# Cross-covariance attention and highway layer in one kernel: twelve tiles of v transposed by DMA, and the last stores ordered in another way

## The chip, the cores and the metric

The kernel runs on one NeuronCore of a Trainium2 chip. The metric is device time in microseconds (us), the median of several executions of the same program. The core has a matrix engine (TensorE, in profiles PE, with its weight loads as PEld), VectorE (DVE), ScalarE (ACT) and GpSimd (POOL); SyncE (SP) mostly issues DMAs. Each engine works through its own instructions in their order and waits on semaphores for the others. All DMAs of the core share 16 DMA engines.

## The reference

For each of four batches of 6336 rows and 256 columns, q and k are normalised along the rows, a 256 x 256 matrix of their products goes through a softmax, and v is multiplied by it; the rows of all batches then go through a highway layer.

```python
B, N, C = (4, 6336, 256)
qn = q / (np.linalg.norm(q, axis=1, keepdims=True) + 1e-06)
kn = k / (np.linalg.norm(k, axis=1, keepdims=True) + 1e-06)
s = kn.transpose(0, 2, 1) @ qn / tau
a = np.exp(s - s.max(-1, keepdims=True))
a /= a.sum(-1, keepdims=True) + 1e-09
x = (v @ a).reshape(B * N, C)
H = np.maximum(x @ w_h, 0.0)
T = 1.0 / (1.0 + np.exp(-(x @ w_t + b_t)))
out = T * H + (1.0 - T) * x
```

Inputs and output are f32; the kernel computes its matrix products in f16 with f32 sums.

## The kernel before

**Tiles.** The rows of a batch are cut into 49 tiles of 128 rows and a rest of 64. A tile takes one row from each partition's stretch, so that a load of several tiles is one long run in each partition. Loads of q, k and v are issued by POOL and cast to f16 on the way; v of the last batch is loaded in four groups of 12, 12, 12 and 13 tiles.

**Two phases, interleaved.** Phase 1 of a batch (`p1_tile`) takes one tile of q and k at a time and adds to two PSUM banks: `S`, the products of k and q, and `G`, the squares on whose diagonals the norms lie. For some tiles of q ACT squares the values instead and DVE adds them up (`squares`, with the places in `SQ_RUNS`). After the last tile of a batch a chain of small steps (`chain`: norms, softmax, and the products of the attention matrix with the two weight matrices) gives `mr`, three 256 x 256 matrices. Its steps are placed at slots by `PLACES`; for the last batch that is `LAST`.

**Phase 2** runs in 100 slots, 25 for each batch, and each slot deals with a pair of tiles of v (the 25th of a batch with the last tile and the rest). A pair needs v transposed, since v is the stationary operand. `transpose` does this on PE: four transposes of 128 x 128 into `vt_bank`, one PSUM bank whose halves the pairs take in turn; `vt_copy` lets DVE copy the result to SBUF (`vts`). Then `mains` makes three groups of four matmuls: `zbank` (the gate), `h` and `x`. ACT takes the sigmoid of the gate into `tt` (`gate_act`) and writes the bias back into the bank for the gate two slots later (`seed`); for the slots in `PE_BIAS` two matmuls on PE do that instead. DVE makes two products, `th` and `ux` (`products`), and POOL subtracts them (`subtract`) into an output tile `o` that holds four slots, in a ring of six. Slots 98 and 99 are subtracted by DVE.

**What sets the order.** The order on each engine is written out by the loop over slots, `for t in range(NSLOT)`. Phase 1 tiles of the next batch are dealt out over the slots; `P1_END` says by which slot a batch must be through, for the last one 63, and from slot 75 on the slots are of the last batch. `TURNS` and `GATES` say in which slots no pair, or two, are transposed or have their gates computed, instead of one: so transposes run three or more slots ahead of `mains`, and gates up to four. A small planner (`note`, `next_loads`, with its constant of 0.305 us for a tile) decides in which slot POOL issues a load.

**Stores.** `subtract` puts a finished output tile into the list `stores`, and `send_store` issues the oldest on SP. Up to `DEFER` stores are kept back, one fewer from each of the slots in `DRAIN` on. A store of 1 MB holds four slots; slots 95 to 98 are stored one by one, 256 KB each, and slot 99 in two parts of 128 and 64 KB. A store is also tied to the latest subtraction that stands before it in the program (`behind`), whatever it holds:

```python
while len(stores) > room and out_now < 2:
    note(send_store(last), now)
    out_now += 1
...
while stores:
    send_store(None)
```

In slot 99 `last` is the subtraction of slot 99 itself, since the loop calls it before it sends the stores.

Of the kernel before, what the change touches and what calls it, by code (L numbers as in the profile page):

```python
# [12 lines left out]
f16 = mybir.dt.float16  # L13
u16 = mybir.dt.uint16

P = 128
# [3 lines left out]
def kernel(  # L20
# [19 lines left out]
    nc = tc.nc  # L40

    B, N, C = q.shape
# [8 lines left out]
    def spans(*sizes):  # L51
        got, s0 = [], 0
        for ns in sizes:
            got.append((s0, ns))
            s0 += ns
        assert s0 == NS
        return got
# [5 lines left out]
    QTILES = 8  # L63
    QRING = 6
    ORING = 6
    DEFER = 5
    DRAIN = [61, 75, 76, 81]
    VG = [spans(6, 10, 12, 12, 9)] + [spans(12, 12, 12, 13)] * (B - 1)
    VTILES = 13
    VALL = [(b, g) for b in range(B) for g in range(len(VG[b]))]  # L70
    VFIRST = [VALL.index((b, 0)) for b in range(B)]
    VRING = 4
    NPAIR = (NS + 1) // 2
# [8 lines left out]
    HEAD = sum(CHAIN0)  # L82
    P1_END = [18, 42, 63]

    GATES = {14: 2, 20: 0, 24: 2, 51: 2, 52: 2, 55: 2, 58: 0, 66: 0, 69: 0, 73: 0, 95: 2}
    TURNS = {50: 1, 51: 2, 52: 2, 59: 1, 61: 2, 64: 0, 70: 0, 73: 0, 93: 2}
    VTS = 9
    OLAST = 2
    TTS = 6

    PE_BIAS = (18, 68, 88, 97)

    DVE_SUBS = (98, 99)

# [2 lines left out]

    SQ_RUNS = {1: (6, 14, 21, 28), 2: (17, 26, 35), 3: (11, 23, 33)}  # L100
    SQ_TILES = 8
    SQ_CUTS = 4
    SQ_RATE = 2
# [1 line left out]

    EARLY = {"sums": (0, "pre"), "norms": (0, "pre"), "invs": (1, "pre"), "cq": (1, "pe"), "logits": (2, "pre"), "exps": (2, "post"), "softmax": (4, "pre"), "at": (4, "pe"), "at_copy": (5, "pre"), "ahat": (5, "pe"), "ahat_copy": (6, "pre")}
    MID = {"sums": (0, "pre"), "norms": (0, "pre"), "invs": (2, "pre"), "cq": (2, "pe"), "logits": (2, "post"), "exps": (3, "post"), "softmax": (3, "post"), "at": (5, "pe"), "at_copy": (6, "pre"), "ahat": (6, "pe"), "ahat_copy": (7, "pre")}
    LAST = {"sums": (0, "pre"), "norms": (0, "pre"), "invs": (2, "pre"), "cq": (2, "pe"), "logits": (2, "post"), "exps": (3, "pre"), "softmax": (6, "pre"), "at": (8, "pe"), "at_copy": (9, "pre"), "ahat": (9, "pe"), "ahat_copy": (10, "pre")}
    PLACES = [None, EARLY, MID, LAST]

    ctx.enter_context(tc.manual_schedule())
    const_pool = ctx.enter_context(tc.tile_pool(name="consts", bufs=1))
    stream_pool = ctx.enter_context(tc.tile_pool(name="stream", bufs=2))
# [9 lines left out]
    q_t, k_t, v_t = {}, {}, {}  # L123
# [76 lines left out]
    def hx_tile(name, shape=(P, 2, C), dt=f32):  # L200
        return psum_pool.tile(list(shape), dt, tag="hx", bufs=3, name=name)
# [39 lines left out]
    def squared(b, j):  # L241

        for n, j0 in enumerate(SQ_RUNS.get(b, ())):
            count = SQ_TILES - (n > 0)
# [10 lines left out]
    def squares(b, j):  # L255
# [24 lines left out]
        add_up(len(cuts))  # L280
        more = n < len(SQ_RUNS[b]) - 1
        if more:
# [12 lines left out]
    def add_up(k):  # L295
        while k > 0 and cuts:
            dst, source = cuts.pop(0)
            nc.vector.tensor_reduce(  # L298
                out=dst, in_=source, op=AluOp.add, axis=mybir.AxisListType.XY
            )  # L300
            k -= 1
# [220 lines left out]
    vT_t = {}  # L522
    vt_bank = psum_pool.tile([P, 2, 2, 2, P], f16, tag="vT", name="vt_bank")
    o_t = {}
    NSLOT = B * NPAIR

    def v_of(b, s):
# [2 lines left out]
        g = max(i for i in range(len(VG[b])) if VG[b][i][0] <= s)  # L530
        return v_t[VFIRST[b] + g][:, s - VG[b][g][0], :]

    def nrows(i):
        return [P, REM] if i == NPAIR - 1 else [P, P]

# [24 lines left out]
    def mains(t, dst, part, seeded):  # L560
        b, i = divmod(t, NPAIR)
        mr = mr_t[b]
        if t in PE_BIAS and seeded:
            for u in range(2):
                nc.tensor.matmul(
                    dst[:, u, :], ones_hl, bt_hl, start=(u == 0), stop=False,
                    skip_group_check=True,
                )
        for u, r in enumerate(nrows(i)):
            for kt in range(2):  # L570
                nc.tensor.matmul(  # L571
                    dst[0:r, u, :], vT_t[t][:, u, kt, 0:r], mr[:, part, kt, :],
                    start=(not seeded and kt == 0 and (u == 0 or i == NPAIR - 1)),
                    stop=(kt == 1 and (u == 1 or i == NPAIR - 1)),
                    skip_group_check=seeded,
                )
# [11 lines left out]
    stores = []  # L588
# [16 lines left out]
    def send_store(behind):  # L605

        tiles, parts = stores.pop(0)
        for dst, src in parts:
            dma = nc.sync.dma_start(out=dst, in_=src)
            if behind is not None:  # L610
                tc.add_manual_dep(
                    dma.ins, behind.ins.name,
                    mybir.DependencyInfo(
                        mybir.DependencyClass.Sync, mybir.DependencyReason.DATA
                    ),
                )
        return tiles
# [3 lines left out]
    def gate_act(s, z):  # L621
        tt_t[s] = work_pool.tile([P, 2, C], f32, tag="tt", bufs=TTS, name=f"tt{s}")
        nc.scalar.activation(out=tt_t[s], in_=z, func=Act.Sigmoid)  # L623

    def seed(s, z):
        if s + 2 < NSLOT and s + 2 not in PE_BIAS:
            nc.scalar.copy(out=z, in_=btb)  # L627
# [34 lines left out]
    def nominal_slot(n):  # L662

        if n < HEAD:
            return -1
        lo, base = RAMP, HEAD
        for i, e in enumerate(P1_END):
            if n < (i + 1) * (NS + 1):
                return lo + (n - base) * (e - lo) // ((i + 1) * (NS + 1) - base)
            lo, base = e + len(LULL) - 1, (i + 1) * (NS + 1)  # L670

    want = []
    for n in range(QFIRST[1] + 1, len(QALL)):
        b, g = QALL[n]
        at = nominal_slot((b - 1) * (NS + 1) + QG[b][g][0])
        for fn, key in ((load_q, "q"), (load_k, "k")):
            want.append((at, len(want), fn, n, ("q", n - QRING), QG[b][g][1]))
    for m in range(2, len(VALL)):
        b, g = VALL[m]
        at = b * NPAIR + VG[b][g][0] // 2 - LOOK - 1  # L680
# [16 lines left out]
    def note(tiles, now):  # L697
        dma_at[0] = max(dma_at[0], now) + tiles * TILE_US
# [96 lines left out]
    now = START_US  # L795
# [46 lines left out]
    def run(t, when):  # L842
        for fn in hooks.pop((t, when), []):
            fn()
# [4 lines left out]
    last = None  # L849
    for t in range(NSLOT):  # L850
        b, i = divmod(t, NPAIR)
        ready = set(used)
        slot[0] = t
        run(t, "pre")
        zs = range(zdone, min(NSLOT, zdone + GATES.get(t, 1)))
        zdone = zs.stop
        turned = range(tdone, min(NSLOT, tdone + TURNS.get(t, 1)))
        tdone = turned.stop
        for s in zs:
            mains(s, zbank[s % 2], 2, True)  # L860
            gate_act(s, zbank[s % 2])
        if pending:
            last = subtract(*pending.pop())
        for s in turned[:1]:
            vt_copy(s, transpose(s))
        for s in zs:
            seed(s, zbank[s % 2])
        h = hx_tile(f"h{t}")
        mains(t, h, 1, False)
        x = hx_tile(f"x{t}")  # L870
        mains(t, x, 0, False)
        for s in turned[1:]:
            vt_copy(s, transpose(s))
        run(t, "pe")
        pending.append((t, *products(t, h, x)))
        add_up(2 if len(cuts) > SQ_RATE else 1)
        run(t, "post")
        for s in turned:
            bb, ii = divmod(s, NPAIR)
            for g, (s0, ns) in enumerate(VG[bb]):  # L880
                if 2 * ii + 2 == s0 + ns or (g == len(VG[bb]) - 1 and ii == NPAIR - 1):
                    used.add(("v", VFIRST[bb] + g))
        if t == NSLOT - 1:
            last = subtract(*pending.pop())


        pb = done1 // (NS + 1)
        count = 0
        for s in turned:
            bb, ii = divmod(s, NPAIR)  # L890
            g = max(g for g in range(len(VG[bb])) if VG[bb][g][0] <= 2 * ii)
            now = max(now, landed.get((load_v, VFIRST[bb] + g), now))
        now += 1.5
        if pb < len(P1_END):
            left = P1_END[pb] - t
            if 0 <= t - end1 < len(LULL):
                due = LULL[t - end1]
            else:
                due = -(-((pb + 1) * (NS + 1) - done1) // left)
            for ahead in range(due):  # L900
                if left > 1 and tile_lands(done1 + ahead) > now + 0.43 * ahead:
                    break
                count += 1
        for _ in range(count):
            pb, j = divmod(done1, NS + 1)
            now = max(now, min(tile_lands(done1), now + 20.0)) + 0.43
            p1_tile(pb + 1, j)
            squares(pb + 1, j)
            done1 += 1
            if j == NS:  # L910
                end1 = t + 1
                steps = chain(pb + 1)
                for name, (at, when) in PLACES[pb + 1].items():
                    hooks.setdefault((t + 1 + at, when), []).append(steps[name])


        if t not in (end1 - 1, end1):
            next_loads(2, now)
        room = DEFER - sum(t >= at for at in DRAIN)
        out_now = 0  # L920
        while len(stores) > room and out_now < 2:
            note(send_store(last), now)
            out_now += 1
        vT_t.pop(t, None)
    while stores:
        send_store(None)
# [36 lines left out]
```

## Time and profile before

| | us |
|---|---|
| median of 5 runs | 275.68 |
| lowest and highest | 275.51, 275.82 |
| the profiled execution, its own time | 275.57 |
| its span, first to last instruction | 273.8 |

The granted TensorE clock was 0.991 on average. The stores are issued by SP; the 1 MB ones take 9.0 us from issue to landing in the middle, and 3.8 us where little else is on the DMA engines (issued at 255.0). The costliest groups of the last stage are, by line, the products `th` (L639) and `ux` (L644) on DVE, POOL's subtraction (L654), and on PE the matmuls of L571 and the transposes of L544.

In the profile an engine's line of digits shows how full it was in each fortieth of the span. A group's line gives line, engine, operation, what is written from what, and the times. In a timeline the first two columns are start and duration in us, and in brackets stands how long the engine had been idle and what ended that. Matmuls overlap, so that the step from one start to the next says more than a duration.

### The profile page before, as it was taken

Reading aid. Unit: us, or ns where it says so; the run is one execution under the profiler, and the core shown is the slowest. Engines: PE = TensorE matmul, PEld = TensorE weight load, DVE = VectorE, ACT = ScalarE, POOL = GpSimd, SP = SyncE. Lnnn points to the kernel's source line nnn. Section 1 sums busy time; section 2 is a strip of 40 time slices with the busy share of each in tenths; the row PEclk is TensorE's granted clock in tenths of the full one; section 3 lists DMA queues with packets and bytes.
Section 4 is the critical chain, followed back from the end, with each engine's and each line's share of the span. In section 5 each row is a group of like instructions: output and inputs, shape, how many; then the busy total and the mean of one; then the engine's idle time right before and its main releaser. Section 6 shows DMA issues by size and latency. Waiting matters only on the chain.

```text
span 273.8 us, 6875 instructions
## 1 busy us (share of the span) xinstructions
PE 253.6 (93%) x2759; PEld 224.9 (82%) x2759; DVE 204.6 (75%) x444; ACT 164.4 (60%) x291; POOL 171.8 (63%) x191
## 2 busy tenths in 40 slices
PE   0679898999999999999999999999999999999990
PEld 0569786999999988899999988899998887999870
DVE  0060046995896876679999767779999999999993
ACT  1030046777772485688675589586645986777750
POOL 6231350899646785628779575609656897888770
PEclk9999999999999999999999999999999999999996
DMA  6999999999999999999999999999999759993366
GB/s 124 212 215 212 210 210 208 214 214 212 215 212 212 215 217 210 236 311 246 286 287 244 305 244 224 219 303 268 279 285 348 154 152 299 423 362 158 156 253 236
DMA packets 16725, 65.64 MB, mean 240 GB/s; under 512 B 1843, under 2 KB 4150, under 8 KB 13750
## 3 DMA queue, kind: packets, MB, share of 16 engines
q0 software_dynamic: 11744, 39.13, 72.2%
q1 hardware_dynamic: 4950, 26.09, 23.9%
q8 instruction: 21, 0.34, 0.5%
q14 instruction: 10, 0.08, 0.1%
HBM read 78.38 MB, written 25.95 MB: 381 GB/s over the span
## 4 chain that ended last, share of the span: by engine, by line
PE 82%; DMA 10%; DVE 3%; issue 1%; ACT 1%; POOL 0%; DVEq 0%; ACTq 0%; POOLq 0%
PE zbank L571 16%; PE h L571 15%; PE x L571 15%; PE S L225 14%; DMA k<-in_k_dram 10%; PE vt_bank L544 8%; PE G L228 7%; PE G L231 4%; PE ah L464 1%; DVE ux L644 1%; DVE th L639 1%; PE sums L320 1%; PE cq L394 1%; DVE vts L557 0%; ACT ssb L417 0%
## 5 line engine op out<-in xcount | busy, mean ns | idle before, releaser
L654 POOL TENSOR_TENSOR o<-th,ux 128x512 f32<-128x512 f32 x95 | 120.6, 1280 | 41.6 <-DVE ux L644 20.4
L571 PEld LDWEIGHTS <-vts 128*128 128x128 f16 x1200 | 110.0, 98 | 14.6 <-issue 3.9
L623 ACT ACTIVATE tt<-zbank 128x512 f32<-128x512 f32 x100 | 59.1, 596 | 55.8 <-PE zbank L571 52.5
L225 PE MATMUL S<-q,k 128*128 128x256 f16 x392 | 81.9, 276 | 10.3 <-DMA k<-in_k_dram 10.3
L228 PE MATMUL G<-k 128*128 128x128 f16 x392 | 73.7, 221 | 0.0
L639 DVE SCALAR_TENSOR_TENSOR th<-h,tt 128x512 f32<-128x512 f32 (+1 forms) x104 | 69.1, 668 | 5.6 <-ACT tt L623 1.0
L644 DVE SCALAR_TENSOR_TENSOR ux<-tt,x 128x512 f32<-128x512 f32 (+1 forms) x104 | 68.1, 658 | 0.0
L571 PE MATMUL h<-mr,vts 128*128 128x256 f16 (+1 forms) x400 | 60.5, 273 | 0.0
L571 PE MATMUL x<-mr,vts 128*128 128x256 f16 (+1 forms) x400 | 60.5, 273 | 0.0
L571 PE MATMUL zbank<-mr,vts 128*128 128x256 f16 (+1 forms) x400 | 59.6, 273 | 0.0
L557 DVE COPY vts<-vt_bank 128x512 f16<-128x512 f16 x96 | 40.4, 421 | 22.9 <-PE vt_bank L544 22.6
L627 ACT COPY zbank<-btb 128x512 f32<-128x512 f32 x94 | 55.2, 592 | 2.7
L225 PEld LDWEIGHTS <-k 128*128 128x128 f16 x392 | 38.8, 99 | 14.7 <-DMA k<-in_k_dram 10.6
L228 PEld LDWEIGHTS <-k 128*128 128x128 f16 x392 | 38.8, 99 | 0.7
L544 PE MATMUL vt_bank<-ident,v 128*128 128x128 f16 x392 | 38.1, 219 | 0.2
L231 PE MATMUL G<-q 128*128 128x128 f16 x246 | 34.4, 222 | 0.0
L544 PEld LDWEIGHTS <-v 128*128 128x128 f16 x392 | 29.9, 98 | 3.3 <-issue 1.1
L129 POOL DMA_DIRECT2D q<-in_q_dram x28 | 15.9, 568 | 18.2 <-DMA q<-in_q_dram 5.8
L135 POOL DMA_DIRECT2D k<-in_k_dram x28 | 15.2, 542 | 16.6 <-DMA k<-in_k_dram 9.3
L273 ACT ACTIVATE sq<-q 128x512 f32<-128x512 f16 (+1 forms) x41 | 23.6, 619 | 0.0
L231 PEld LDWEIGHTS <-q 128*128 128x128 f16 x246 | 19.3, 100 | 1.6
L298 DVE TENSOR_REDUCE sq<-sq 128x64 f32<-128x512 f32 x28 | 18.0, 680 | 0.0
(100 smaller groups left out, 120.5 us busy)
## 6 DMA issues: line engine op xcount, KB each, us to landing
out_dram<-o SPq DMA_DIRECT2D x23, 1024.0 KB, 9.0
q<-in_q_dram POOLq DMA_DIRECT2D x20, 512.0 KB, 16.9
k<-in_k_dram POOLq DMA_DIRECT2D x20, 512.0 KB, 17.8
v<-in_v_dram POOLq DMA_DIRECT2D x11, 768.0 KB, 18.8
v<-in_v_dram POOLq DMA_DIRECT2D x3, 832.0 KB, 26.2
out_dram<-o SPq DMA_DIRECT2D x4, 256.0 KB, 2.3
q<-in_q_dram POOLq DMA_DIRECT2D x3, 320.0 KB, 17.4
k<-in_k_dram POOLq DMA_DIRECT2D x3, 320.0 KB, 17.0
```

What stands on the lines that cost most here:

```text
L225: nc.tensor.matmul(S[:, c, :], kc, qq[0:nr, :], start=first and c == 0, stop=last and c == 1)
L228: nc.tensor.matmul(G[:, c, :], kc, kc, start=first and c == 0, stop=False)
L231: nc.tensor.matmul(G[:, 2 + c, :], qc, qc, start=False, stop=last and c == 1)
L273: nc.scalar.activation(out=sq[:, o // 2, :, u : u + src.shape[1]].rearrange("p c u -> p u c"), in_=src, func=Act.Square,)
L544: nc.tensor.transpose(ps[:, u, c, 0 : nr[u]], vt[0 : nr[u], bass.ts(c, P)], ident[0 : nr[u], 0 : nr[u]],)
L557: nc.vector.tensor_copy(out=sb, in_=ps)
L571: nc.tensor.matmul(dst[0:r, u, :], vT_t[t][:, u, kt, 0:r], mr[:, part, kt, :], start=(not seeded and kt == 0 and (u == 0 or i == NPAIR - 1 ...
L623: nc.scalar.activation(out=tt_t[s], in_=z, func=Act.Sigmoid)
L627: nc.scalar.copy(out=z, in_=btb)
L639: nc.vector.scalar_tensor_tensor(out=th[pr, us, :], in0=h[pr, us, :], scalar=0.0, in1=tt[pr, us, :], op0=AluOp.max, op1=AluOp.mult,)
L644: nc.vector.scalar_tensor_tensor(out=ux[pr, us, :], in0=tt[pr, us, :], scalar=1.0, in1=x[pr, us, :], op0=AluOp.subtract, op1=AluOp.mult,)
L654: last = eng.tensor_tensor(out=ot[pr, o0 + us.start : o0 + us.stop, :], in0=th[pr, us, :], in1=ux[pr, us, :], op=AluOp.subtract,)
```

## The change

Two groups of six tiles of v of the last batch, tiles 26 to 31 and 38 to 43 (pairs 88 to 90 and 94 to 96), are no longer transposed by PE and copied by DVE. In slots 78 and 79 SP issues one DMA transpose for each, from the tile of v in SBUF into a tile in the rings of q and k, and the pairs' matmuls read that tile. In slots 98 and 99 stores are no longer tied to the latest subtraction, only to their own data; the last store, the 64 rows of the rest, is issued by ACT. Several constants move: the slots of `DRAIN`, `GATES`, `TURNS` and `PE_BIAS`, the first run of squares of the last batch, and the softmax of the last batch by one slot.

On the engines PE has 24 transposes and their weight loads fewer, DVE six copies fewer, SP two DMA transposes more and a store fewer, and ACT a store more. On SP the first transpose stands after the store of o62 and before that of o66, the second between those of o66 and o70.

```diff
-    DRAIN = [61, 75, 76, 81]
+    DRAIN = [57, 78, 74, 84]
...
-    GATES = {14: 2, 20: 0, 24: 2, 51: 2, 52: 2, 55: 2, 58: 0, 66: 0, 69: 0, 73: 0, 95: 2}
-    TURNS = {50: 1, 51: 2, 52: 2, 59: 1, 61: 2, 64: 0, 70: 0, 73: 0, 93: 2}
+    GATES = {17: 2, 20: 0, 27: 2, 51: 2, 52: 2, 55: 2, 58: 0, 66: 0, 69: 0, 73: 0, 95: 2}
+    TURNS = {49: 2, 51: 2, 52: 2, 53: 0, 59: 1, 60: 2, 64: 0, 72: 0, 73: 0, 93: 2}
...
-    PE_BIAS = (18, 68, 88, 97)
+    TGROUPS = ((26, 6, 78), (38, 6, 79))
+
+    PE_BIAS = (18, 21, 83, 97)
...
-    SQ_RUNS = {1: (6, 14, 21, 28), 2: (17, 26, 35), 3: (11, 23, 33)}
+    SQ_RUNS = {1: (6, 14, 21, 28), 2: (17, 26, 35), 3: (9, 23, 33)}
...
-    LAST = {"sums": (0, "pre"), "norms": (0, "pre"), "invs": (2, "pre"), "cq": (2, "pe"), "logits": (2, "post"), "exps": (3, "pre"), "softmax": (6, "pre"), "at": (8, "pe"), "at_copy": (9, "pre"), "ahat": (9, "pe"), "ahat_copy": (10, "pre")}
+    LAST = {"sums": (0, "pre"), "norms": (0, "pre"), "invs": (2, "pre"), "cq": (2, "pe"), "logits": (2, "post"), "exps": (3, "pre"), "softmax": (7, "pre"), "at": (8, "pe"), "at_copy": (9, "pre"), "ahat": (9, "pe"), "ahat_copy": (10, "pre")}
...
+    BY_DMA = {}
+
+    def dma_transposes(t):
+
+        for n, (s0, ns, at) in enumerate(TGROUPS):
+            if at != t:
+                continue
+            g = max(g for g in range(len(VG[B - 1])) if VG[B - 1][g][0] <= s0)
+            o = s0 - VG[B - 1][g][0]
...
+            vt = stream_pool.tile(
+                [P, QTILES, C], f16, tag="qk"[n % 2] + "_in", bufs=QRING, name=f"vtd{n}"
+            )
+            nc.sync.dma_start_transpose(
+                out=vt[:, 0:ns, :].rearrange("p s (c r) -> p (s c) r", c=2),
+                in_=v_t[VFIRST[B - 1] + g][:, o : o + ns, :].rearrange("p s c -> p (s c)"),
+            )
+            note(3.5 * ns, 0.0)
+            for j in range(0, ns, 2):
+                vT_t[(B - 1) * NPAIR + (s0 + j) // 2] = vt[:, j : j + 2, :].rearrange(
+                    "p u (c r) -> p u c r", c=2
+                )
+
+    for s0, ns, _ in TGROUPS:
+        for i in range(s0 // 2, (s0 + ns) // 2):
+            BY_DMA[(B - 1) * NPAIR + i] = True
...
         tiles, parts = stores.pop(0)
-        for dst, src in parts:
-            dma = nc.sync.dma_start(out=dst, in_=src)
+        for n, (dst, src) in enumerate(parts):
+
+            ends = n == 1 and not stores and behind is None
+            dma = (nc.scalar if ends else nc.sync).dma_start(out=dst, in_=src)
...
+        dma_transposes(t)
+        by_pe = [s for s in turned if s not in BY_DMA]
...
-        for s in turned[:1]:
+        for s in by_pe[:1]:
             vt_copy(s, transpose(s))
...
-        for s in turned[1:]:
+        for s in by_pe[1:]:
             vt_copy(s, transpose(s))
...
-            note(send_store(last), now)
+            note(send_store(last if t < NSLOT - 2 else None), now)
```

More of the change, by code (lines that the diff above doesn't have):

```diff
@@ L531, in v_of @@
         return v_t[VFIRST[b] + g][:, s - VG[b][g][0], :]
+    BY_DMA = {}
[5 more added lines that the diff above has]
+            o = s0 - VG[B - 1][g][0]
+            assert o + ns <= VG[B - 1][g][1] and s0 % 2 == 0 and ns % 2 == 0
+            vt = stream_pool.tile(
[13 more added lines that the diff above has]
+            BY_DMA[(B - 1) * NPAIR + i] = True
     def nrows(i):
```

## The prediction

> **What bounds the kernel now.** I read the page's busy times and slices first, to see which engine is full and when.
>
> ```profile
> PE 253.6 (93%) x2759; PEld 224.9 (82%) x2759; DVE 204.6 (75%) x444; ACT 164.4 (60%) x291; POOL 171.8 (63%) x191
> ...
> PE   0679898999999999999999999999999999999990
> ...
> DVE  0060046995896876679999767779999999999993
> ...
> PE 82%; DMA 10%; DVE 3%; issue 1%; ACT 1%; POOL 0%; DVEq 0%; ACTq 0%; POOLq 0%
> ```
>
> PE is full from the third slice to the one before the last, and 82% of the chain that ended last is PE. VectorE (DVE) is full as well in the last twelve slices, so what is taken from PE there pays only if DVE gives way too. Next the table by stretches, for the stage that the transposes leave.
>
> ```profile
> core 0: us, PE busy (x) PEld busy (x) DVE busy (x) ACT busy (x) POOL busy (x), PEclk, DMA share, GB/s
> 236.00:240.00 4.00, 4.00 (x45) 3.64 (x43) 4.00 (x9) 3.28 (x6) 3.24 (x4) 1.00 1.01 426
> 244.00:248.00 4.00, 4.00 (x43) 3.61 (x42) 4.00 (x9) 2.64 (x5) 3.24 (x4) 1.00 0.47 194
> 252.00:256.00 4.00, 4.00 (x43) 3.63 (x42) 4.00 (x10) 3.12 (x6) 3.29 (x3) 1.00 0.10 39
> ```
>
> PE and DVE have no idle time; the DMA engines (column before the last) are full until 240 and have room after 244. Then PE and DVE in order of time around slots 93 and 94.
>
> ```profile
> 255.52 0.60 PE L571 MATMUL zbank<-mr,vts 128*128 128x256 f16 x4
> 255.95 0.39 PE L544 MATMUL vt_bank<-ident,v 128*128 128x128 f16 x4
> 256.18 0.60 PE L571 MATMUL h<-mr,vts 128*128 128x256 f16 x4
> 256.61 0.60 PE L571 MATMUL x<-mr,vts 128*128 128x256 f16 x4
> 257.05 0.38 PE L544 MATMUL vt_bank<-ident,v 128*128 128x128 f16 x4
> 257.27 0.60 PE L571 MATMUL zbank<-mr,vts 128*128 128x256 f16 x4
> 257.95 0.38 PE L544 MATMUL vt_bank<-ident,v 128*128 128x128 f16 x4
> ```
> ```profile
> 256.58 0.42 DVE L557 COPY vts<-vt_bank 128x512 f16<-128x512 f16 x1
> 257.48 0.42 DVE L557 COPY vts<-vt_bank 128x512 f16<-128x512 f16 x1 [0.47 <-PE vt_bank L544]
> 257.81 0.68 DVE L639 SCALAR_TENSOR_TENSOR th<-h,tt 128x512 f32<-128x512 f32 x1
> ```
>
> Starts on PE are 0.44 us apart for four matmuls and 0.22 or 0.23 for four transposes (255.95 to 256.18): a slot takes 3 x 0.44 + 0.22 = 1.53 us. Slot 93 turns two pairs; the transposes at 257.95 start when the copy of 257.48 is over, so z's 0.44 from 257.27 is followed by 0.24 us of idle PE. Last the end.
>
> ```profile
> 262.56 0.69 DVE L639 SCALAR_TENSOR_TENSOR th<-h,tt 128x512 f32<-128x512 f32 x1 [0.24 <-PE h L571]
> 263.88 0.69 DVE L639 SCALAR_TENSOR_TENSOR th<-h,tt 128x512 f32<-128x512 f32 x1
> ...
> 268.66 0.75 DVE L654 TENSOR_TENSOR ol<-th,ux 128x256 f32<-128x256 f32 x2
> ```
> ```profile
> 269.44 0.81 SPq L609 DMA_DIRECT2D out_dram<-o  x2
> 270.30 0.95 SPq L609 DMA_DIRECT2D out_dram<-ol  x2
> ```
>
> A slot with no transpose lasts 1.32 us (262.56 to 263.88). PE ends at 266.9, DVE's serial tail at 269.41, and only 0.03 later do four stores leave SP one after another; two of them hold slots 97 and 98, whose data were ready at 266.5 and 267.4. The last is issued at 270.78, lands at 272.77 (2.0 us, by the landings of the tile `ol`), and 1.03 us later the span ends.
>
> **The change part by part.** *PE.* Six pairs lose four transposes each: 6 x 0.22 = 1.32 us, in slots 85, 86, 87, 91, 92 and one of slot 93's two. It lies on the path, as PE has no idle time there. *DVE* loses six copies, 0.34 us apart from the next start (253.51 to 253.85): 2.0 us. Without them a DVE slot is 1.20 us (`th` 0.60, `ux` 0.60, start to start), POOL's subtraction 1.28, ACT's sigmoid and copy 0.60 + 0.59 = 1.19: all under 1.32, so the smaller saving, PE's, counts. *Slot 93* keeps one pair, so nothing waits for a second copy: 0.24 us more.
>
> *The last stores.* Slots 97 and 98 go out on their own subtractions, off the path. The first half of the last pair leaves SP when its own subtraction ends, 0.34 before DVE's end, and at the 2.27 us of such a store (270.30 to 272.57) lands 1.93 after it. The second half is issued by ACT. No row shows ACT issuing a DMA; SP issues a store in 0.33 to 1.25 us, with landings of 2.0 to 2.3 from the issue for these sizes. Nothing excludes either end; I take SP's 2.0 with 0.05 for the semaphore (ACT has ended at 265.4 and has nothing queued), and 1.2 us more for the range. Last landing after DVE's end: 2.05 instead of 3.36, so 1.31 us less.
>
> *The DMA transposes.* Two instructions on SP, each 128 x 1536 of f16, 384 KB. They are costed at nothing on the path; their cover is the time until their readers. SP reaches the first right after the store of o62, which waits for slot 74's subtraction (230.2); its load of v landed at 219.3, and the q and k slots that it overwrites were last read in phase 1. On the rings it stands behind o54, o58 and o62, which land at 233.3, 236.8 and 239.2 in the run of before; so its data start at 239.2. Reader: z of slot 88, at 247.85 now, less 3 x 0.22: 247.2. The second is queued behind the store of o66, which waits for slot 77's subtraction (234.8), and on the rings behind the first and that store's 2.4 us (236.8 to 239.2). Reader: z of slot 94, at 257.27 less 1.32: 256.0. With T for one transpose, they land at 239.2 + T and 241.6 + 2T; the first is late beyond T = 8.0, the second beyond 7.2.
>
> T appears in no row. From below: 384 KB at a store's 2.4 us per MB, 0.9 us. From above: 1536 rows of 256 bytes, each at the 60 ns of the trace's 512-byte packets, over 16 engines: 5.8 us. Farther still, each of 196,608 elements as one of the 4-byte packets (20 ns): 246 us, and the kernel would lose hundreds; but whole rows of 256 bytes are what lies side by side in the source, so the 512-byte packet is nearest. I take 5.8 (the planner's own allowance in the diff, 3.5 x 6 tiles x 0.305, comes to 6.4): landings at 245.0 and 253.2, over 2 us early each. Behind them o66 lands by 247.4, o70 by 255.6; POOL needs their buffers in slots 91 and 95 (255.3 and 262.5 now). SP's later stores wait for later subtractions anyway.
>
> [...] On PE the trace has 0.22 us for four transposes, 55 ns each. [...]
>
> *The moved steps* (z's runs ahead in GATES, places in TURNS, DRAIN, softmax of the last batch, runs of squares, two bias slots) keep their counts: four bias pairs, 22 squared tiles, the same stores. They hide under PE, which is full from 62 us on; DRAIN's later stores are covered by POOL's ring of six tiles. If the cover is gone somewhere, the price is one ACT square or seed copy, 0.6 us, at each place; PE's remaining gaps (0.27 at 212.6, 0.19 at 217.5) bound a gain by 0.5. I take zero.
>
> Sum against the profiled execution's own 275.57 us (span 273.8 and 1.8 around it): 1.32 + 0.24 + 1.31 = 2.87, so 272.70; the median of the runs is 0.11 above that execution: 272.8.
>
> **The rivals.** *The transposes land late* (the other side). PE stops at z of slot 94, and POOL after it for o70's buffer. Net it is slower once 241.6 + 2T passes 256.0 by 2.87, at T = 8.6 us, 90 ns a row. At 120 ns a row, T = 11.5: 8.6 us late, 275.7 - 2.9 + 8.6 = 281.4. For it: T was never seen, and the rings are full when it is queued. Against: DMA's share is 0.47 and 0.10 after 244, and the nearest packet is 60 ns. *Another engine takes PE's place* in the slots without transposes, POOL with its 1.28 and a 0.25 wait for `ux` being closest: then only the stores pay, 275.7 - 1.3 = 274.4. For it: the margin is 0.04; against: POOL runs two subtractions in 2.51 us. *ACT's store is slow*: 1.2 of the 1.31 is lost, 274.0. *A moved step stalls PE* in an earlier phase, z's lead over slots 14 to 16 above all, where ACT has squares queued: one or two times 0.6, 273.4 to 274.0.
>
> **How the numbers follow.** Forecast 0.57; late transposes 0.14; another engine 0.11; ACT's store 0.08; a moved step 0.10. The forecast's own range is 272.2 (PE's other gaps close) to 273.3. With the three milder rivals the range ends at 274.7; what is left out above is nearly all late transposes. About 0.2% (0.55 us) is what a measurement of this kernel can tell from no change. Slower takes late transposes but for 0.01, so 0.13; same 0.03 from that and from mixtures of the milder rivals; faster the rest, 0.84.
>
> **What would show it.** Right: a PE step of 1.32 us in slots 85 to 87, 91 and 92, transposes landing before z of 88 and 94, no 0.24 gap in slot 94, DVE's end at 267.9, the last landing 2 us after it. Wrong: PE waiting for `vtd`, starts 1.5 us apart in those slots, an ACT issue over 1 us, or new PE gaps before 224.

## The result, and the profile after

| | before | after |
|---|---|---|
| median, runs of one comparison (us) | 275.52, 37 runs | 274.97, 19 runs |
| lowest and highest | 275.16, 275.85 | 274.67, 275.33 |
| ratio of the two, 95% interval | | 0.998 [0.9973, 0.9986] |
| the profiled execution, its own time | 275.57 | 274.93 |
| its span | 273.8 | 273.2 |

The changed kernel is 0.55 us faster, where 2.8 us were predicted; 274.97 lies above the upper end of the prediction's range, 274.7. The page of the changed kernel first:

```profile
PE 253.0 (93%) x2735; PEld 224.2 (82%) x2735; DVE 202.9 (74%) x438; ACT 164.4 (60%) x291; POOL 171.6 (63%) x191
...
PE   0689898999999999999999999999999999999990
...
DVE  0060036996896876578999867689998999999983
...
PE 80%; DMA 10%; DVE 5%; ACT 1%; issue 1%; POOL 0%; DVEq 0%; ACTq 0%; POOLq 0%
```

PE has the 24 transposes fewer (2759 to 2735), yet its busy time fell by 0.6 us only, and the part of DVE in the chain that ended last rose from 3% to 5%. Matmuls overlap (in the timeline of slot 94 below a group of four takes 0.60 us, and the next starts 0.44 after its start), so a busy time does not show small pauses; the starts do. The next table is worked out from the traces: the start of the first matmul of `h` in a slot, after less before.

| slot | 0 to 13 | 20 | 21 | 27 to 45 | 68 | 73 to 82 | 83 | 88 | 91 | 93 | 94 to 99 |
|---|---|---|---|---|---|---|---|---|---|---|---|
| us | -0.02 | -0.02 | +0.20 | +0.57 | +0.58 | +0.98 | +1.20 | +0.31 | +0.09 | -0.13 | -0.60 |

From slot 82 to slot 94 the changed kernel gains 1.58 us; the prediction had 1.32 + 0.24 = 1.56. (The 0.22 lost at slot 83 and given back at slot 88 is a bias pair on PE that moved from the one to the other.) Ahead of slot 82 it loses 1.00. So the first surprise lies where no transpose was taken away. The stretches that the prediction showed, with the mean DMA share as the last column but one:

```profile
core 0: us, PE busy (x) PEld busy (x) DVE busy (x) ACT busy (x) POOL busy (x), PEclk, DMA share, GB/s
244.00:248.00 4.00, 4.00 (x39) 3.59 (x38) 3.80 (x7) 3.44 (x6) 3.56 (x3) 1.00 1.08 316
252.00:256.00 4.00, 4.00 (x41) 3.59 (x39) 3.93 (x8) 3.43 (x6) 3.40 (x4) 1.00 0.46 188
```

PE is as full as before, DVE nearly (3.80 and 3.93 of 4.00). The DMA engines now have at 244 and at 252 what they did earlier in the kernel before (shares of 0.47 and 0.10 there), since SP's stores stand behind the two DMA transposes. SP's queue and the tile that the transposes write, in the timeline (start, duration) and by the tile (durations in ns, first and last start):

```profile
229.02 2.84 SPq L641 DMA_DIRECT2D out_dram<-o  x3
232.16 6.12 SPq L549 DMA_TRANSPOSE vtd<-v  x1
238.40 0.99 SPq L641 DMA_DIRECT2D out_dram<-o  x1
239.62 4.16 SPq L549 DMA_TRANSPOSE vtd<-v  x1
...
268.50 0.33 SPq L641 DMA_DIRECT2D out_dram<-ol  x1
```
```profile
L601 PE MATMUL zbank<-mr,vtd x24: 272/272/273, 248.2 to 259.2; 128*128 128x256 f16 x24
...
DMA to landing us min/median/max: 9.5/9.5/9.5
```

The first transpose, issued at 232.16, has landed 9.5 us later, at 241.65; its reader starts at 248.2. How long the transfers themselves took stands in the trace's records of DMA packets, of which these two alone have 256 bytes (1536 each): the first's run from 238.08 to 241.18, which is 3.10 us, the second's from 243.41 to 245.96, 2.55 us, where the prediction assumed 5.8. (The first landing follows that of the store of o62, ahead of it, by 1.44 us; that is no duration, as the first packets run 2.1 us before the store has landed, at 240.21.) The second's reader starts at 256.91. What is long is the issue: SP is occupied for 6.12 and 4.16 us. Slot 94 on PE, and the tail on DVE and ACT:

```profile
256.04 0.60 PE L601 MATMUL h<-mr,vts 128*128 128x256 f16 x4
256.48 0.60 PE L601 MATMUL x<-mr,vts 128*128 128x256 f16 x4
256.91 0.60 PE L601 MATMUL zbank<-mr,vtd 128*128 128x256 f16 x4
257.35 0.39 PE L574 MATMUL vt_bank<-ident,v 128*128 128x128 f16 x4
257.57 0.60 PE L601 MATMUL h<-mr,vtd 128*128 128x256 f16 x4
```
```profile
268.06 0.75 DVE L686 TENSOR_TENSOR ol<-th,ux 128x256 f32<-128x256 f32 x2
```
```profile
268.84 0.55 ACTq L641 DMA_DIRECT2D out_dram<-ol  x1
```

After z at 256.91 the transposes start 0.44 later, with no idle time between. DVE ends at 268.81, ACT issues the last store 0.03 later, in 0.55, and it lands at 270.85: 2.04 after DVE's end, as predicted (2.05). But the span ends at 273.16, 2.31 after that landing, where it was 1.00 in the kernel before. That is the second surprise.

No view shows what lies there, as busy times leave out the engines' own closing instructions; the records of the trace have them. When the work is over, every engine has a closing DRAIN instruction (in the kernel before 0.61 us on ACT, 0.81 on PE, 0.67 on DVE, 7.78 on POOL, 0.01 on SP), and SP goes through the semaphores that the landings raise, one wait after another (ten waits from 271.31 to 272.82); then all meet (from 273.03 on, when POOL's DRAIN is over). The table has, for each kernel, the last subtraction on POOL, POOL's closing DRAIN, the last landing, the end of SP's waits, and the end of the span (us; kernels e1 to e15 follow below).

| kernel | last subtraction on POOL | its DRAIN: start + duration = end | DVE's end | last landing | SP's waits over | span ends | less the later of the two |
|---|---|---|---|---|---|---|---|
| before | 265.24 to 266.52 | 265.21 + 7.78 = 272.98 | 269.41 | 272.77 | 272.86 | 273.77 | 0.79 |
| after | 264.64 to 265.91 | 264.61 + 7.77 = 272.37 | 268.81 | 270.85 | 271.83 | 273.16 | 0.79 |
| e1 | 263.90 to 265.17 | 263.86 + 7.77 = 271.63 | 268.06 | 270.12 | 271.10 | 272.42 | 0.79 |
| e3 | 265.75 to 267.02 | 265.71 + 7.77 = 273.48 | 269.91 | 272.21 | 272.47 | 274.26 | 0.78 |
| e4 | 263.49 to 264.76 | 263.45 + 7.76 = 271.22 | 267.66 | 271.03 | 271.79 | 272.63 | 0.84 |
| e9 | 264.57 to 265.84 | 264.53 + 7.76 = 272.30 | 268.74 | 270.79 | 270.94 | 273.09 | 0.79 |
| e10 | 262.92 to 264.18 | 262.88 + 7.76 = 270.64 | 268.78 | 270.89 | 271.05 | 271.89 | 0.84 |
| e13 | 262.17 to 263.44 | 262.14 + 7.77 = 269.91 | 268.03 | 270.06 | 270.22 | 271.06 | 0.84 |
| e15 | 262.78 to 264.05 | 262.74 + 7.77 = 270.51 | 268.65 | 271.96 | 272.05 | 272.89 | 0.84 |

POOL's DRAIN, whose record starts 0.03 to 0.04 us ahead of its last subtraction, lasts 7.76 to 7.78 us in every kernel, and the span ends 0.78 to 0.79 after it or 0.83 to 0.85 after SP's waits, whichever ends later. In the kernel before both ended within 0.12 us of each other, so the landing of the last store looked like the cause of the end. In the changed kernel the store lands 1.92 us earlier, and POOL's DRAIN ends only 0.61 earlier, as its last subtraction starts 0.60 earlier.

### The profile page after: what moved, and what is told of

It reads as the page before. It is cut to its first block, busy times and chain, and to the rows that moved or that the text cites. A ratio compares the mean times of both kernels' runs of the same rounds, so it can differ in the third digit from the quotient of the medians.

```text
span 273.2 us, 6827 instructions
## 1 busy us (share of the span) xinstructions
PE 253.0 (93%) x2735; PEld 224.2 (82%) x2735; DVE 202.9 (74%) x438; ACT 164.4 (60%) x291; POOL 171.6 (63%) x191
## 4 chain that ended last, share of the span: by engine, by line
PE 80%; DMA 10%; DVE 5%; ACT 1%; issue 1%; POOL 0%; DVEq 0%; ACTq 0%; POOLq 0%
PE zbank L601 15%; PE h L601 15%; PE x L601 15%; PE S L227 14%; DMA k<-in_k_dram 10%; PE vt_bank L574 7%; PE G L230 7%; PE G L233 4%; DVE th L671 2%; DVE ux L676 1%; PE ah L466 1%; PE sums L322 1%; ACT ssb L419 0%; ACT tt L655 0%; DVE vts L587 0%
## 5 line engine op out<-in xcount | busy, mean ns | idle before, releaser
L601 PEld LDWEIGHTS <-vts 128*128 128x128 f16 x1128 | 103.6, 98 | 13.9 <-issue 4.0
L601 PE MATMUL h<-mr,vts 128*128 128x256 f16 (+1 forms) x376 | 56.9, 273 | 0.0
L601 PE MATMUL x<-mr,vts 128*128 128x256 f16 (+1 forms) x376 | 56.9, 273 | 0.0
L601 PE MATMUL zbank<-mr,vts 128*128 128x256 f16 (+1 forms) x376 | 56.2, 273 | 0.1
L587 DVE COPY vts<-vt_bank 128x512 f16<-128x512 f16 x90 | 37.8, 420 | 23.4 <-PE vt_bank L574 23.1
L574 PE MATMUL vt_bank<-ident,v 128*128 128x128 f16 x368 | 35.8, 219 | 0.2 <-DVE vts L587 0.2
L574 PEld LDWEIGHTS <-v 128*128 128x128 f16 x368 | 27.9, 98 | 3.4 <-issue 1.4
```

The costliest lines, as they stand in the source:

```text
L574: nc.tensor.transpose(ps[:, u, c, 0 : nr[u]], vt[0 : nr[u], bass.ts(c, P)], ident[0 : nr[u], 0 : nr[u]],)
L587: nc.vector.tensor_copy(out=sb, in_=ps)
L601: nc.tensor.matmul(dst[0:r, u, :], vT_t[t][:, u, kt, 0:r], mr[:, part, kt, :], start=(not seeded and kt == 0 and (u == 0 or i == NPAIR - 1 ...
```

## The experiments

Four kernels take the change apart. *Theory D* says that POOL's DRAIN, or SP's waits if they are later, sets the end; *theory P* that the moved places cost PE 1 us ahead of slot 83. The rivals to both stand in the expectations.

**e1: the transposes and the stores, with the six constants as before.**

```diff
-    DRAIN = [57, 78, 74, 84]
+    DRAIN = [61, 75, 76, 81]
...
-    PE_BIAS = (18, 21, 83, 97)
+    PE_BIAS = (18, 68, 88, 97)
...
(GATES, TURNS, SQ_RUNS and LAST likewise)
```

> The changed kernel with the six moved constants set back (DRAIN, GATES, TURNS, PE_BIAS, squares, softmax), transposes and stores as changed. Theory P (the moved places cost about 1.0 us of PE before slot 83): h of slot 82 starts 0 to 0.1 us from where it started in the kernel before (239.1), and the time is 274.0, about 1.0 under the changed kernel. Rival Q (the drift before slot 83 has another cause, such as the stores or chance): h of slot 82 at 240.0 again and the time is 275.0. In both the end after the last landing takes over 1.8 us.

Measured 274.19 us, ratio 0.9946 [0.9933, 0.9958]. The start of `h` stands at +0.23 us against the kernel before in slot 0 and at +0.24 in slot 82: no loss on the way. From there to slot 94 it gains 1.59.

**e2: the kernel before with the six constants moved, and nothing else.** (The same lines with the signs the other way round.)

> The kernel before with the six moved constants alone. Theory P: about 1.0 us slower than before (276.5), with h of slot 82 at 240.0. Rival Q: within 0.2 us of before.

Measured 276.84, ratio 1.0046 [1.0033, 1.0058]: slower. The start of `h` goes from -0.10 in slot 0 to +0.89 in slot 82, the same 0.99 as in the changed kernel, but for 0.01. e1 and e2 together show that the constants alone make the first loss. In e2 another 0.36 is lost at slot 94; no run says by what.

**e3: the kernel before with the stores of the change alone.**

```diff
+            ends = n == 1 and not stores and behind is None
+            dma = (nc.scalar if ends else nc.sync).dma_start(out=dst, in_=src)
...
-            note(send_store(last), now)
+            note(send_store(last if t < NSLOT - 2 else None), now)
```

> The kernel before with the changed stores alone (slots 97 and 98 tied to their own data, the last store on ACT). Theory R (the closing sequence gives back what the stores gain): DVE ends at 269.4, the last landing comes at 271.5 instead of 272.8, but the span ends over 1.8 us after the landing instead of 1.0, so the time is 275.1 to 275.6. Rival S (the long end of the changed kernel was chance): 1.0 us after the landing, time 274.2.

Measured 275.75, ratio 1.0002 [0.9993, 1.0011]: no change. The last landing came 2.30 us after DVE's end instead of 3.36, and the end 2.05 after the landing instead of 1.00; the table has POOL's DRAIN ending 1.0 us after SP's waits.

**e4: the kernel before with the DMA transposes alone** (`TGROUPS`, `dma_transposes`, `by_pe`).

> The kernel before with the DMA transposes alone, stores and places as before. The PE saving of 1.32 and the gap of 0.24 are collected in full: DVE ends at 267.8, the end follows 3.36 + 1.03 us later, time 274.0. Rival (transposes cost something elsewhere, say on the DMA engines or in POOL's waits): 274.5 or more.

Measured 274.55, ratio 0.9964 [0.9952, 0.9976]; half a microsecond over the expectation and on the rival's side of it. The start of `h` gains 1.58 as in e1, so nothing is lost on PE. But two DMAs more on SP shift which semaphores the last stores raise, and SP, which goes through its closing waits in a fixed order, still had some to go through when the last store landed, with a pause of 0.47 us among them: its waits were over 0.76 after the landing, against 0.09 in the kernel before. So the end was SP's here: the cost elsewhere that the rival spoke of is in SP's closing waits, and not on the DMA engines, as the last landing comes 3.37 us after DVE's end, as before (3.36).

### What ends the span

**e5: e1 with slot 97's subtraction on DVE,** so that POOL's last one is that of slot 96.

```diff
-    DVE_SUBS = (98, 99)
+    DVE_SUBS = (97, 98, 99)
```

> The old places with transposes and stores as changed, and slot 97's subtraction given to DVE, so that POOL's last instruction is slot 96's. Theory D (the end waits for the later of two things: POOL's closing drain, which ends 7.77 us after its last subtraction starts, and SP's last landing with the waits behind it): POOL's drain still lasts 7.8 us and ends at about 270.3 instead of 271.6, DVE ends 0.4 to 0.6 later, and SP's waits (0.47 of stalled instructions and nine waits of 0.06 after the landing) take over: 274.0 to 274.4, no gain on 274.2. Rival E (POOL's drain is only idle time that ends when the others are done): the drain's end moves with SP's, not with POOL's last subtraction.

Measured 273.91, ratio 0.9939 [0.9926, 0.9953], against e1's 0.9946: no gain that these intervals tell from none. The profiled execution took 926.1 us, so its trace has no such table; but even there POOL's DRAIN lasts 7.76 us, and it ends 8.8 us ahead of SP's waits. A DRAIN that ended when the others are done (rival E) would not. **e6 and e7** were to take both bounds apart: the six stores of batch 0 in halves, which moves the last stores on to the last semaphores of SP's list, without and with e5's edit.

```diff
+            if b == 0 and t < 24:
+                stores.append((2 * OG, [
+                    (rows(ob)[:, s0 : s0 + OG, :], ot[:, 0:OG, :]),
+                    (rows(ob)[:, s0 + OG : s0 + 2 * OG, :], ot[:, OG : 2 * OG, :]),
+                ]))
+            else:
```

> The old places with transposes and stores as changed, and the six 1 MB stores of the first batch sent in halves, so that the last two stores raise the last two of SP's eight semaphores. Theory D: SP is done 0.1 us after the last landing, but POOL's drain ends as late as before (7.77 us after slot 97's subtraction starts), so 274.1 to 274.3 again. Rival F (SP's waits alone set the end): about 1.0 us less, 273.2.

> Both edits together: slot 97's subtraction on DVE and the semaphores turned. Theory D: SP's last landing at about 270.7 is followed by 0.8 to 1.0 us, span 271.6, time 273.2 to 273.5, about 0.8 under either edit alone. Rival F: the same as the turned semaphores alone plus the 0.5 that DVE's end loses.

Measured 275.77, ratio 1.0007 [0.9998, 1.0016], and 275.11, ratio 0.9981 [0.9972, 0.9989]. Both came out 1.5 to 1.9 us over what theory D expected, for a reason of their own, which costs PE 2.12 and 1.85 us at slot 31. POOL waits for the first output tile's store, and PE behind it (e6):

```profile
124.23 3.72 POOL L692 TENSOR_TENSOR o<-th,ux 128x512 f32<-128x512 f32 x3 [8.64 <-DMA out_dram<-o]
```
```profile
126.27 0.60 PE L601 MATMUL x<-mr,vts 128*128 128x256 f16 x4 [1.96 <-DVE th L677]
```

POOL idles 8.64 us for that buffer (5.20 in e1), and PE is 1.96 us idle for `th`. e7 against e6 still says what was asked: 0.66 us less, with the end 0.98 after the last landing instead of 1.78.

**e9 and e10** make the same step without that cost: SP's three small loads of the bias at the start become one, so that two DMAs fall away on SP.

```diff
-    for r in (0, 32, 64):
-        nc.sync.dma_start(out=bt_sb[r : r + 1, :], in_=moe_b_t.rearrange("(a m) -> a m", a=1))
+    nc.sync.dma_start(
+        out=bt_sb[0:65:32, :],
+        in_=moe_b_t.rearrange("(a m) -> a m", a=1).to_broadcast([3, C]),
+    )
```

> The six constants as before, both halves of the change kept (this is e1), and the three one-row loads of the bias at the start made into one load of three rows. SP then issues two transfers fewer, so the last two stores raise the last semaphores of the closing list instead of its third and fourth, without the cost that the split stores of e6 had in slot 31. Theory D (the closing drain of POOL, 7.77 us from the start of its last subtraction, ends the span 0.75 us later, whichever of it and SP's waits is later): as e1, 274.2 us, since POOL's drain was at 271.63 there; SP's waits end some 0.3 to 0.5 us after the last landing, before POOL. Rival W (SP's waits behind the last landing set the end): 0.5 us less than e1, 273.7.

> e9 with slot 97's subtraction on DVE too (DVE_SUBS 97, 98, 99), so that POOL's last subtraction is that of slot 96. Theory D: POOL's drain starts 1.3 us earlier; DVE ends some 0.5 us later (e7 against e6), and the end follows the last landing by 1.0 us (e7: 0.98) instead of 2.3 in e1: 0.7 us less than e9 (e7 was 0.66 under e6), 273.5 us. Theory W: the end moves with DVE's end, 0.5 us more than e9.

Measured 274.38, ratio 0.9956 [0.9942, 0.9969], and 273.67, ratio 0.993 [0.9917, 0.9942]. e9's time alone would not decide, since e9 and e10 also have a pause on DVE that costs 0.36 us at slot 24 (next part). The trace does: in e9 SP's waits are over 0.15 after the landing, against 0.98 in e1, and the span ends as late as in e1, 2.30 after it. Rival W falls. In e10 POOL's DRAIN ends before SP's waits, and the kernel is 0.71 us faster, as theory D has it. The end of POOL's work on the timeline, in the changed kernel and in e13 (e10 with one memset more, below):

```profile
261.86 1.28 POOL L686 TENSOR_TENSOR o<-th,ux 128x512 f32<-128x512 f32 x1 [0.77 <-POOL o L686]
263.33 2.58 POOL L686 TENSOR_TENSOR o<-th,ux 128x512 f32<-128x512 f32 x2 [0.20 <-DVE ux L676]
```
```profile
260.69 1.28 POOL L690 TENSOR_TENSOR o<-th,ux 128x512 f32<-128x512 f32 x1 [0.77 <-POOL o L690]
262.17 1.27 POOL L690 TENSOR_TENSOR o<-th,ux 128x512 f32<-128x512 f32 x1 [0.20 <-DVE ux L680]
```

The first ends with two subtractions (x2), the second with one: the DRAIN starts a subtraction earlier.

### What the moved places cost

Two of the places where the changed kernel loses can be seen in its timelines. Around 107 us, DVE and PE of the changed kernel:

```profile
106.31 0.42 DVE L587 COPY vts<-vt_bank 128x512 f16<-128x512 f16 x1 [0.48 <-PE vt_bank L574]
107.22 0.69 DVE L671 SCALAR_TENSOR_TENSOR th<-h,tt 128x512 f32<-128x512 f32 x1 [0.48 <-PE x L601]
```
```profile
106.98 0.60 PE L466 MATMUL ah<-wht,at_sb 128*128 128x256 f16 x4
107.96 0.60 PE L466 MATMUL ah<-wht,at_sb 128*128 128x256 f16 x4 [0.38 <-DVE th L671]
```

and DVE of the kernel before:

```profile
106.11 0.42 DVE L557 COPY vts<-vt_bank 128x512 f16<-128x512 f16 x1 [0.48 <-PE vt_bank L544]
106.65 0.69 DVE L639 SCALAR_TENSOR_TENSOR th<-h,tt 128x512 f32<-128x512 f32 x1
```

`th` starts 0.54 after the start of the copy before, and 0.91 after it in the changed kernel, although its last input, by the matmuls, was there at 106.8; PE waits 0.38 us behind it. In six traces (the changed kernel, e2, e9, e10, e11, e12) such a pause, 0.47 to 0.48 us with nothing to wait for, stands ahead of the 192nd record of DVE's instruction stream, waits included, and in each that record is `th`. In ten others one record more stands ahead; the 192nd is a wait that starts 0.02 us after the end of the copy, and `th` is not late. *Theory G* is a pause at a fixed place of the stream, which in those ten would run beside the copy; that it is there is inferred, not seen. e9 and e10 have the pause with the old places, e1 has not: e1 and e9 differ in SP's loads of the bias alone, so it is the number of records ahead that counts, and not which work they do.

**e8: the changed kernel with one small memset more on DVE at the start.**

```diff
+    spare = const_pool.tile([P, 4], f32, tag="spare")
+    nc.vector.memset(spare, 0.0)
```

> The changed kernel with one small memset more on DVE at the start, where DVE is idle. Theory G (DVE's instruction stream stalls about 0.45 us at a fixed place, its 191st instruction, and the moved places have brought the product th of slot 23 to it): th of slot 23 starts about 0.1 us after its h instead of 0.5, slot 27 is 0.35 to 0.4 us earlier, and the time is 274.6 instead of 275.0. Rival H (th of slot 23 waits for x by some order that the places bring): no difference, 275.0.

Measured 274.54, ratio 0.9959 [0.9946, 0.9971], 0.43 us under the changed kernel, by an instruction more. `th` follows the copy at once again:

```profile
106.46 0.42 DVE L589 COPY vts<-vt_bank 128x512 f16<-128x512 f16 x1 [0.48 <-PE vt_bank L576]
107.00 0.69 DVE L673 SCALAR_TENSOR_TENSOR th<-h,tt 128x512 f32<-128x512 f32 x1
```

The other place is the softmax of the last batch, on ACT and, in the second view, in the chain that ended last of the changed kernel:

```profile
220.06 0.59 ACT L659 COPY zbank<-btb 128x512 f32<-128x512 f32 x1
221.32 0.91 ACT L440 ACTIVATE mr<-ssb,rinv 128x256 f16<-128x256 f32 x2 [0.67 <-DVE rinv L436]
222.13 0.57 ACT L655 ACTIVATE tt<-zbank 128x512 f32<-128x512 f32 x1
222.74 0.59 ACT L659 COPY zbank<-btb 128x512 f32<-128x512 f32 x1
```
```profile
220.61 0.53 DVE ux L676
...
221.32 0.91 ACT mr L440 x2
222.22 0.49 ACT tt L655
222.74 0.60 ACT zbank L659
223.38 0.60 PE zbank L601 x4
```

The softmax, one slot later, has ACT wait 0.67 us for `rinv`, which DVE computes only behind `ux` (from 221.14); the sigmoid and the bias copy queued behind it are late, and PE's gate waits for that copy until 223.38. ACT, 60% busy on the page, is on the path here.

**e11 and e12** set places of the changed kernel back, first the bias pairs alone, then `TURNS` and the softmax.

```diff
e11:
-    PE_BIAS = (18, 21, 83, 97)
+    PE_BIAS = (18, 68, 88, 97)
e12:
-    TURNS = {49: 2, 51: 2, 52: 2, 53: 0, 59: 1, 60: 2, 64: 0, 72: 0, 73: 0, 93: 2}
+    TURNS = {50: 1, 51: 2, 52: 2, 59: 1, 61: 2, 64: 0, 70: 0, 73: 0, 93: 2}
...
-    LAST = {... "softmax": (7, "pre"), ...}
+    LAST = {... "softmax": (6, "pre"), ...}
```

> The changed kernel with the places of the four bias pairs alone set back (18, 68, 88, 97). Theory P (moved places cost 1 us of PE ahead of slot 83, each its own part): the 0.22 us at slot 21 is gone, and 0.22 at slot 68 comes in its place but partly into idle time of PE: 0.0 to 0.2 us under the changed kernel, 274.8 to 275.0. Rival (the bias places are the whole loss of 1 us): 274.0.

> The changed kernel with the turns of the transposes (TURNS) and the place of the last batch's softmax set back. Theory P: the 0.4 us lost in slots 69 to 73 comes back, the pauses at slots 21 and 24 to 27 stay: 274.5 to 274.6 us. Rival (the loss in slots 69 to 73 comes from the bias pair or z's leads and not from these two): as the changed kernel, 274.97.

e11: 275.02, ratio 0.9981 [0.9971, 0.999], as the changed kernel: the 0.22 saved at slot 21 is lost again in slots 67 to 69. e12: 274.42, ratio 0.996 [0.9948, 0.9973], 0.55 us less; the start of `h` stays at +0.56 to +0.60 from slot 66 to 82, where the changed kernel goes from +0.57 to +0.98. The turns and the softmax were set back together, so that it is the softmax that matters is read from the traces and not shown by a run of its own. ACT no longer waits (e12):

```profile
220.61 0.91 ACT L440 ACTIVATE mr<-ssb,rinv 128x256 f16<-128x256 f32 x2
221.42 0.57 ACT L655 ACTIVATE tt<-zbank 128x512 f32<-128x512 f32 x1
222.02 0.59 ACT L659 COPY zbank<-btb 128x512 f32<-128x512 f32 x1
```

**e14: e8's memset and e12's places together,** to see whether the two pieces add up.

> The changed kernel with e8's memset and with e12's older turns and softmax. Theory: the two losses of PE are separate and are nearly all of the 1 us, so their gains add: 274.97 less 0.43 (e8) less 0.55 (e12), 274.0 us, with a drift of PE against the kernel before of 0.1 us or less at slot 82. Rival (both give back the same piece): 274.4 us, as e12 alone.

Measured 274.20, ratio 0.9949 [0.9936, 0.9961], e1's time again (0.9946). The start of `h` goes from +0.04 in slot 0 to +0.24 in slot 82; of the 1.00 us, 0.80 are these two, and 0.20 are left, a little over the expectation. The two are not quite separate: alone, e8 takes 0.52 of the loss away and e12 0.45, and both take away the same 0.16 at slot 69. The 0.20 appear in slot 21, where a bias pair now stands on PE (+0.22); the pair taken from slot 68 gives 0.22 back around slot 65 that is lost in the slot after.

### What the stores are worth, and the best version

**e13** is e10 with the memset of e8, as e10 has the pause at `th` as well; **e15** is e13 with the stores of the kernel before.

```diff
e15:
-            ends = n == 1 and not stores and behind is None
+            ends = False
...
-            note(send_store(last if t < NSLOT - 2 else None), now)
+            note(send_store(last), now)
```

> e10 with one small memset on DVE at the start (as e8), a candidate for the best version. Theory G (DVE pauses 0.45 us at a fixed place of its instruction stream; in e10, as in the changed kernel, that place is th of slot 23, which costs 0.37 us of PE in slot 24): the memset moves the pause under the copy before it, 0.37 us less than e10, 273.3 us. Rival (that pause is made by the work around slot 23): as e10, 273.67.

> e13 with the stores as in the kernel before: all held to the last subtraction, all from SP. Theory D (the edit of the stores shows once POOL's drain is out of the way): the last landing is 3.36 us after DVE's end instead of 2.05 (as before against the changed kernel), so 1.0 to 1.3 us over e13, 274.3 to 274.6 us. Rival (the edit of the stores is worth nothing in itself): as e13.

e13: 273.14 us, ratio 0.9909 [0.9895, 0.9922], 0.5 under e10 and the fastest of all. e15: 274.24, ratio 0.995 [0.9937, 0.9964]. In e15 the last landing comes 3.31 us after DVE's end, in e13 2.03, and both spans end 0.93 to 1.00 after it: with POOL's DRAIN out of the way the edit of the stores is worth 1.1 us, and without that, nothing (e3).

## Why the prediction was wrong

*PE in the last stage: right.* 1.58 us gained for 1.56 forecast, in the slots named, with steps of 0.22 and the gap of slot 94 gone; e4 shows it alone. So no other engine took PE's place.

*The DMA transposes: right that they cost nothing, their size wrong.* T came out at 3.10 and 2.55 us for 5.8 assumed, between the bounds of 0.9 and 5.8: a packet of 256 bytes took 30 ns in the mean, where the row that the prediction took had 60. So the transfers run at 127 and 154 GB/s. Both transposes were there before their readers. The 6.12 and 4.16 us in which SP only issues them were in no term; that they cost nothing was luck, as the stores behind them had that much room (POOL waits for no store's buffer from 225 us on).

*The last stores: the landing right, its use wrong.* 2.04 us after DVE's end for 2.05 forecast, and ACT's issue was 0.55. The step that failed reads "and 1.03 us later the span ends": it was taken for a constant behind the last landing. The end is that of POOL's DRAIN, 7.77 us from the start of its last subtraction, or of SP's waits, and in the kernel before the two were 0.12 apart. So the 1.31 us were not on the path (e3: 1.0002), and only where POOL's DRAIN ends earlier does the edit get 1.1 of them (e13 against e15). The rival "ACT's store is slow" had the loss, 1.2 of the 1.31, and not its cause.

*The moved steps: wrong.* The step that failed reads "They hide under PE, which is full from 62 us on [...] I take zero." The cover was the wrong way round: a full PE is what a late input delayed here (by 0.38 us behind `th` at 107.96). They cost 1.00 us ahead of slot 83 (e2 alone, e1 without). About 0.4 come in slots 69 to 73, with ACT's wait in the last batch's softmax and the turns next to it, about 0.4 are DVE's pause, 0.2 a bias pair. The rival "a moved step stalls PE" had the mechanism and a fair price, one or two times 0.6, but looked for it in slots 14 to 16, where PE gained 0.44 and gave it back in slot 17.

The sum against the profiled execution, then: 1.32 + 0.24 as forecast, less 1.00, and 0 for 1.31, is 0.6; its own time fell by 0.64. The rivals were priced one at a time. Here two losses came together, 1.00 on the way and 1.31 at the end (272.8 + 2.3 = 275.1), and the range's upper end of 274.7 had no room for that.

## What to carry to other kernels

Before a store at the end is paid for, look at what else must be over: an engine's last instruction and its closing drain can end as late as the last landing (272.98 and 272.77 in the kernel before), and then both must go. A constant that moves work by one slot is an edit with a price of its own, to be read where that work waits for another engine and at what is queued behind it; the busy share of the engine (ACT, 60%) doesn't tell. Test the parts of a change that promise nothing by themselves first: here they took back two thirds of what the others gained on PE.

## What the runs showed of the hardware

- POOL's closing DRAIN lasts 7.76 to 7.78 us in all seventeen traces; its record starts 0.03 to 0.04 us ahead of POOL's last subtraction, which takes 1.26 to 1.28. It ends before SP's waits in e4, e7, e10, e13 and e15 and after them in e1, e3 and e9, and lasts the same. No run tells what it waits for.
- Pauses at a fixed place of an instruction stream: DVE's ahead of its 192nd record, 0.47 to 0.48 us where it can be seen, and SP's ahead of its 80th, 0.45 to 0.50 us in fifteen traces and longer in the two others (e3, e9). An instruction more or fewer ahead moves the work under them; one useless memset was worth 0.43 us. What makes the pauses was not examined.
- SP's waits were over 0.98 us after the last landing in the changed kernel, where that pause (270.90 to 271.36) and most of its list of semaphores came after the landing, and 0.15 in e9, where two DMAs fewer had put both ahead of it.
- A DMA transpose of 384 KB takes 2.0 to 5.3 us from its first packet to its last, beside the packets of stores (thirteen traces, e5 left out; 3.10 and 2.55 in the changed kernel); its issue occupies SP for 2.1 to 8.0 us in these runs.
